# Key-value sums of four heads per product, both signs on the 128 rows and 65 columns, and one slab that reads out from normalized, transposed queries

## The chip, the cores and the metric

The kernel runs on one core of a Trainium2 chip. The metric is the device time of one launch in microseconds, as a median over several runs. A profiler has recorded one execution of the kernel before. The engines are named as the profile names them: PE is the matrix engine, PEld its weight loads, DVE, ACT and POOL are the vector, scalar and GpSimd engines, and SP is the engine whose queue issues most transfers.

## The reference, cut to what matters

The input x has 2048 rows of 512 numbers. Four blocks are added to it in turn, each on a layer-normalized x: linear attention (called layer 0), a gated feed-forward block (layer 1), attention again (layer 2), and the feed-forward block again (layer 3). Both attentions use the same weights, and so do both feed-forward blocks.

```
pq, pk  = q @ w_phi, k @ w_phi                       # 32 heads of 16 numbers each
phi_q   = concat(softmax(pq), softmax(-pq))          # 32 features per head
phi_k   = concat(softmax(pk), softmax(-pk))
kv      = sum over rows of phi_k[f] * v[d]           # 32 x 16 per head
z       = sum over rows of phi_k[f]
o       = (phi_q @ kv) / (phi_q @ z + 1e-6)
x       = x + o @ wo
x       = x + (relu(y @ W_gate) * (y @ W_up)) @ W_down     # 1376 columns between
```

## The kernel before

The 2048 rows are 16 tiles t of 128 rows, and four tiles make a slab s. Each operation is declared with its engine, its reads and writes and an assumed cost; a planner orders the operations on each engine once, by a stored list of ranks (`RANKS`) and a list of operations that go to their other engine (`MOVED`). On the chip each engine, and each DMA queue (that of SP among them), works off its own list strictly in that order and waits on semaphores. A burst of matmuls declared as one operation raises its semaphore once, at its end.

At the start, PE transposes the key and query weights (`turn`, line 579, four operations of four transposes for each, with four copies out of PSUM by ACT or DVE for each), and `compose` multiplies them with the block-diagonal w_phi. So there are weights `Wkp` and `Wqp` that give pk and pq straight from y.

`ln` (line 612) normalizes a tile to y and transposes it to yT, mostly with a DMA transpose on SP's queue (line 654).

`kv_tile(l, t)` (line 661) makes the features of the keys of one tile: four matmuls of 512 columns (lines 672 and 676), two exponentials by ACT (line 683), sums over groups of 16 by DVE (line 692; for the tiles in `POOL_Z` by POOL and DVE, lines 688 and 689), the reciprocal (line 700, or lines 697 and 698 on ACT) and the multiplication `norm` on DVE (line 701). Tile `ft` holds all 512 positive features and then all 512 negative ones. The values take four more matmuls (line 710) and one copy.

`kv_sums(l)` (line 737) multiplies the features with the values. A group is one sign and eight heads: 128 feature columns are the stationary side, and 128 value columns with one column of ones, 129, the moving side.

```
i = e.matmul(pt.ap()[:, j * 144:j * 144 + 129], ph[l, t][0].ap()[:, s, c * 128:(c + 1) * 128], va[l, t][0].ap()[:, c, 0:129],
```

That is eight matmuls per tile, 128 per attention layer. Of the products only the blocks in which the head of the feature is the head of the value are kept, by a mask in lines 753 and 756, into `kvs` (8 groups of 144 columns).

`q_chunk(l, s, c)` (line 718) makes the query's features for 128 feature columns and all 512 rows of a slab, already transposed (features on the partitions, line 725), and exponentiates them with both signs (line 729). They are not normalized.

`attn_tile(l, t)` (line 762) reads out: eight matmuls of 144 columns (line 778), of which 16 columns give the denominators and the softmax sums of the query. ACT copies these (line 792), POOL or DVE combines them (lines 799, 801, 805) with a logarithm and an exponential on ACT between (lines 803, 804), DVE scales the two signs apart (lines 815, 820), DVE or POOL adds them (lines 824, 825), the result is transposed (line 831 by PE, line 836 by a DMA) and multiplied with wo (line 841), and DVE adds it to x (line 844).

`glu_slab` and `gate_col` (line 857) make the feed-forward block's hidden columns for a slab (lines 871, 878, 879), `rem` (line 883) its last 96 columns, and `down` (line 911) the product with W_down for one tile (lines 925, 927, 933). After `down(1, t)` the kernel declares `ln(2, t)` and `kv_tile(2, t)`, so that the keys of layer 2 are made while layer 1 is still at work. All query chunks of layer 2 are declared after that.

Of the kernel before, what the change touches and what calls it, by code (L numbers as in the profile page):

```python
# [421 lines left out]
def build_kernel(nc, A_x, A_wqkv, A_w_phi, A_wo, B_x, B_W_gate, B_W_up, B_W_down, out):  # L422
# [28 lines left out]
    kvs = sb("kvs", [8, 144])  # L451
# [5 lines left out]
    p_ph = ring("phik", 16, [2, 512])  # L457
    p_va = ring("vaug", 16, [NC, 130])
    p_eq = ring("expq", 22, [512])
    p_hT = ring("hT", 22, [512])  # L460
# [7 lines left out]
    p_z = ring("z", 4, [64], FP32)  # L468
    p_rz = ring("rz", 4, [64])
# [121 lines left out]
    if ("sp", "wqn") in LOADS or ("pool", "wqn") in LOADS:  # L591
        turn(lambda ic: wqn[:, ic, :], lambda ic: [c_wqn, c_wd], t_wq, c_wqT, "WqT", ["act", "dve", "act", "dve"])
# [64 lines left out]

    ph, va = {}, {}
    kop = {}

    def kv_tile(l, t):
        src, rr = yT[l, t // 4], res("yT", l, t)
        c0 = (t % 4) * 128
        kt, kr = tile(p_ps, "K", l, t)
        ft, fr = tile(p_ph, "ph", l, t)
        zt, zr = tile(p_z, "z", l, t)
        rt, rzr = tile(p_rz, "rz", l, t)
        ph[l, t] = (ft, fr)

        def mmk(e):  # L670
            for ic in range(4):
                i = e.matmul(kt.ap(), src.ap()[:, ic, c0:c0 + 128], Wkp[:, ic, :], start=(ic == 0), stop=(ic == 3))  # L672
            return i
        if (l, t) == (0, 0):
            for ic in range(4):
                o = op("pe", lambda e, ic=ic: e.matmul(kt.ap(), src.ap()[:, ic, c0:c0 + 128], Wkp[:, ic, :], start=(ic == 0), stop=(ic == 3)),
                       reads=[rr, r_wk[ic]], writes=[kr], claims=[ft], ii=216, lat=382, name=f"K{l}.{t}")
            kop[l, t] = o
        else:
            kop[l, t] = op("pe", mmk, reads=[rr] + r_wk, writes=[kr], claims=[ft], ii=864, lat=1030, name=f"K{l}.{t}")  # L680
        fr2 = [Res("phh", ft), Res("phh", ft)]
        for s in range(2):
            op("act", lambda e, s=s: e.activation(ft.ap()[:, s, :], kt.ap(), ACT.Exp, scale=(1.0, -1.0)[s]), reads=[kr], writes=[fr2[s]], ii=477, lat=600, name=f"expk{l}.{t}")  # L683
        if (l, t) in POOL_Z:
            ht_, hr_ = tile(p_t, "zh", l, t)
            zh = lambda: ht_.ap().rearrange("p a b -> p (a b)").bitcast(FP32)
            v = lambda: ft.ap().rearrange("p s (a f b) -> p (s a) f b", f=16, b=2)
            op("pool", lambda e: e.tensor_tensor(zh().rearrange("p (a b f) -> p a f b", f=8, b=2), v()[:, :, 0:8, :], v()[:, :, 8:16, :], ALU.add), reads=fr2, writes=[hr_], ii=1110, lat=1154, name=f"Zp{l}.{t}")
            op("dve", lambda e: e.tensor_reduce(zt.ap(), zh().rearrange("p (q f) -> p q f", f=8), AX.X, ALU.add), reads=[hr_], writes=[zr], ii=590, lat=670, name=f"Zh{l}.{t}")
            zr = [zr]  # L690
        else:
            op("dve", lambda e: e.tensor_reduce(zt.ap().rearrange("p (a b) -> p a b", b=2), ft.ap().rearrange("p s (a f b) -> p (s a) b f", f=16, b=2), AX.X, ALU.add),  # L692
               reads=fr2, writes=[zr], ii=1105, lat=1185, name=f"Z{l}.{t}")
            zr = [zr]
        if (l, t) in ACT_RZ:
            lz = Res("lz", zt)
            op("act", lambda e: e.activation(zt.ap(), zt.ap(), ACT.Ln), reads=zr, writes=[lz], ii=150, lat=260, name=f"lZ{l}.{t}")
            op("act", lambda e: e.activation(rt.ap(), zt.ap(), ACT.Exp, scale=-1.0), reads=[lz], writes=[rzr], ii=150, lat=260, name=f"rZa{l}.{t}")
        else:
            op("dve", lambda e: e.reciprocal(rt.ap(), zt.ap()), reads=zr, writes=[rzr], ii=420, lat=526, name=f"rZ{l}.{t}")  # L700
        op("dve", lambda e: e.tensor_tensor(ft.ap().rearrange("p s (a f b) -> p (s a) f b", f=16, b=2), ft.ap().rearrange("p s (a f b) -> p (s a) f b", f=16, b=2),  # L701
                                            rt.ap().rearrange("p (a b) -> p a b", b=2).unsqueeze(2).to_broadcast([P, 32, 16, 2]), ALU.mult),
           reads=fr2 + [rzr], writes=[fr], ii=602, lat=695, name=f"norm{l}.{t}", port=True)
        vt, vr = tile(p_ps, "V", l, t)
        at, ar = tile(p_va, "va", l, t)
        va[l, t] = (at, ar)

        def mmv(e):
            for ic in range(4):
                i = e.matmul(vt.ap(), src.ap()[:, ic, c0:c0 + 128], wv[:, ic, :], start=(ic == 0), stop=(ic == 3))  # L710
            return i
        op("pe", mmv, reads=[rr, c_wv], writes=[vr], claims=[at], ii=864, lat=1030, name=f"V{l}.{t}")
        op_copy("act", lambda: at.ap()[:, :, 0:128], lambda: vt.ap().rearrange("p (c n) -> p c n", c=4), [vr] + ([res("va1", i) for i in range(16)] if l == 0 else []), [ar], f"va{l}.{t}", False)


    eq = {}
# [14 lines left out]


    GROUPS = [[(0, 0), (0, 1), (0, 2)], [(1, 0), (1, 1), (1, 2)], [(0, 3), (1, 3)]]
    kvr = {}
    BURSTS = [(0, 4), (4, 8), (8, 12), (12, 14), (14, 15), (15, 16)]

    def kv_sums(l):
        for b, gs in enumerate(GROUPS):
            pt, pres = tile(p_ps, "kv", l, b)
            n = len(gs)  # L740
            for q, ts in enumerate(BURSTS):
                def mm(e, gs=gs, ts=ts, pt=pt):
                    for t in range(*ts):
                        for j, (s, c) in enumerate(gs):
                            i = e.matmul(pt.ap()[:, j * 144:j * 144 + 129], ph[l, t][0].ap()[:, s, c * 128:(c + 1) * 128], va[l, t][0].ap()[:, c, 0:129],  # L745
                                         start=(t == 0 and j == 0), stop=(t == 15 and j == len(gs) - 1), skip_group_check=True)
                    return i
                k = (ts[1] - ts[0]) * n
                op("pe", mm, reads=[ph[l, t][1] for t in range(*ts)] + [va[l, t][1] for t in range(*ts)], writes=[pres], ii=k * 58, lat=k * 58 + 166, name=f"kv{l}.{b}.{q}",
                   after=[kop[l, 12]])  # L750
            g = b * 3
            src = lambda pt, n: pt.ap()[:, 0:n * 144].rearrange("p (j w) -> p j w", w=144)
            op("dve", lambda e, g=g, n=n, pt=pt: e.tensor_tensor(kvs[:, g:g + n, 0:128].rearrange("p j (h d) -> p j h d", h=8), src(pt, n)[:, :, 0:128].rearrange("p j (h d) -> p j h d", h=8),
                                                                 mask2[:].unsqueeze(1).unsqueeze(3).to_broadcast([P, n, 8, 16]), ALU.mult),
               reads=[pres, c_m2], writes=[res("kvsn", b)], ii=70 + n * 132, lat=150 + n * 132, name=f"kvs{l}.{b}")
            op("dve", lambda e, g=g, n=n, pt=pt: e.scalar_tensor_tensor(kvs[:, g:g + n, 128:136], src(pt, n)[:, :, 128:129].to_broadcast([P, n, 8]), 5e-7,
                                                                        mask2[:].unsqueeze(1).to_broadcast([P, n, 8]), ALU.add, ALU.mult),
               reads=[pres, c_m2], writes=[res("kvsd", b)], ii=90, lat=180, name=f"kvsd{l}.{b}")
        kvr[l] = [[res("kvsn", b), res("kvsd", b), res("kvsm")] for b in range(3)]


    def attn_tile(l, t):
        s4, tt = t // 4, t % 4
        st_, sr = tile(p_sm, "sm", l, t)
# [8 lines left out]
        for b, gs in enumerate(GROUPS):  # L773
            pt, pres = rb[b]

            def mm(e, gs=gs, pt=pt, b=b):
                for j, (s, c) in enumerate(gs):
                    i = e.matmul(pt.ap()[:, j * 144:(j + 1) * 144], eq[l, s4, c, s][0].ap()[:, tt * 128:(tt + 1) * 128], kvs[:, b * 3 + j, :], start=True, stop=True)  # L778
# [29 lines left out]
        for b, gs in enumerate(GROUPS):  # L808
# [16 lines left out]
           alt=("pool", lambda e: e.tensor_tensor(ot_.ap(), tt_.ap()[:, 0, :], tt_.ap()[:, 1, :], ALU.add), 1015.0, 1060.0))  # L825
        if (l, t) in PE_O:
# [6 lines left out]
            op("pe", mmt, reads=[or_] + c_id, writes=[pres], ii=230, lat=400, name=f"oTp{l}.{t}")  # L833
            op_copy("act", lambda: oT_.ap(), lambda pt=pt: pt.ap().bitcast(BF16)[:, 0:512].rearrange("p (k n) -> p k n", k=4), [pres], [oTr], f"oTcp{l}.{t}", True)
        else:
            op("sp", lambda e: e.dma_start_transpose(oT_.ap(), ot_.ap()), reads=[or_], writes=[oTr], dma="tr", nbytes=500, name=f"oT{l}.{t}")
# [105 lines left out]
    for i in range(16):  # L942
        op("pool", lambda e, i=i: e.memset(va_all[i][:, :, 128:130], 1.0), writes=[res("va1", i)], ii=60, name="vones", after=[yop[0, 0]])
# [4 lines left out]
    op("pool", lambda e: e.tensor_copy(kvs[:, :, 136:144], mask2[:].unsqueeze(1).to_broadcast([P, 8, 8])), reads=[c_m2], writes=[res("kvsm")], ii=200, lat=280, after=[kop[0, 8]], name="kvsm")  # L948
# [13 lines left out]
    for l in (0, 2):  # L962
        for s in range(NS):
            for c in range(4):
# [5 lines left out]
        for s in range(NS):  # L970
# [3 lines left out]
            for t in range(4 * s, 4 * s + 4):  # L974
                down(l + 1, t, last=(l == 2))
                if l == 0:
                    ln(2, [t])
                    kv_tile(2, t)
    pr.first([kop[0, t] for t in range(FIRST)], 1e5)
# [135 lines left out]
```

## Time and profile before

| quantity | value |
|---|---|
| median of 4 runs | 389.25 us (388.61 to 390.22) |
| the profiled execution | 388.61 us |
| its span, first to last instruction | 386.8 us |
| around the span (worked out) | 1.8 us |
| granted PE clock, mean | 1.000 |
| busy: PE, DVE, ACT, POOL | 378.0, 294.8, 195.5, 57.4 us |

A matmul's row in the profile gives its duration from start to end, and successive matmuls overlap. The time that a matmul costs PE in a stream is therefore the distance between starts: a burst's length less one duration, divided by the number of matmuls less one. Busy shares of the other engines can be read directly. The profile's tables of windows give the busy time of each engine in a stretch, in microseconds and with the number of instructions in brackets.

### The profile page before, as it was taken

The numbers are of one execution on the slowest core, as the hardware profiler recorded it, in microseconds if no ns is written. First come the engines' busy times: TensorE is split into PE (matmuls) and PEld (weight loads), VectorE is DVE, ScalarE is ACT, GpSimd is POOL, SyncE is SP. The second block draws the span as 40 slices with busy tenths as digits, with TensorE's granted clock in tenths as the row PEclk, the third lists the DMA queues.
The fourth block names the chain that finished last, engine by engine and source line by source line (L and its number), as shares of the span: only waits on it lengthen the run. The fifth ranks groups of instructions, "written<-read, shape, count | busy, mean of one in ns | idle before, by whom it ended". The sixth has DMA issues, their size and how long they took to land.

```text
span 386.8 us, 6635 instructions
## 1 busy us (share of the span) xinstructions
PE 378.0 (98%) x2430; PEld 214.0 (55%) x2471; DVE 294.8 (76%) x646; ACT 195.5 (51%) x609; POOL 57.4 (15%) x129
## 2 busy tenths in 40 slices
PE   8999899999999999999999999999999999999997
PEld 6545575787554544444444467587565454444443
DVE  7999977999997886663798986899867784643443
ACT  6999859664253236243256675875342343123210
POOL 1377301213112000000000000222201020100000
PEclk9999999999999999999999999999999999999999
DMA  8542951223232222010030100022330221210101
GB/s 254 157 97 43 297 196 30 43 55 70 54 70 54 44 54 41 15 27 2 0 69 2 27 2 1 15 43 54 70 82 18 65 56 27 74 36 14 42 14 54
DMA packets 60592, 22.89 MB, mean 59 GB/s; under 512 B 51760, under 2 KB 60304, under 8 KB 60560
## 3 DMA queue, kind: packets, MB, share of 16 engines
q1 hardware_dynamic: 57440, 19.35, 22.1%
q10 hardware_dynamic: 2832, 2.08, 1.7%
q0 software_dynamic: 288, 1.05, 0.8%
q8 instruction: 19, 0.31, 0.3%
q14 instruction: 13, 0.11, 0.1%
HBM read 8.44 MB, written 2.10 MB: 27 GB/s over the span
## 4 chain that ended last, share of the span: by engine, by line
PE 76%; DVE 10%; ACT 8%; DMA 3%; issue 1%; POOL 1%; SPq 1%; POOLq 0%
PE pb L871 32%; PE pb L925 17%; PE pb L841 5%; PE pb L725 5%; PE pb L672 4%; PE pb L710 4%; PE pb L745 3%; ACT phik L683 3%; PE pb L778 3%; PE pb L899 2%; ACT expq L729 2%; PE pb L927 2%; DVE phik L701 2%; DMA Wd<-in_A_wqkv_dram 2%; DVE t L815 1%
## 5 line engine op out<-in xcount | busy, mean ns | idle before, releaser
L878 ACT ACTIVATE gate<-pb 128x512 bf16<-128x512 f32 (+1 forms) x100 | 51.1, 512 | 76.6 <-PE pb L871 73.7
L879 DVE TENSOR_TENSOR hT<-gate,pb 128x512 bf16<-128x512 bf16 (+1 forms) x100 | 56.9, 577 | 39.3 <-PE pb L871 36.8
L871 PE MATMUL pb<-yT,Wu 128*128 128x512 bf16 (+1 forms) x396 | 82.6, 336 | 0.2
L871 PE MATMUL pb<-yT,Wg 128*128 128x512 bf16 (+1 forms) x393 | 81.7, 336 | 0.5
L925 PE MATMUL pb<-Wd,hT 128*128 128x512 bf16 (+2 forms) x322 | 75.5, 372 | 0.5
L871 PEld LDWEIGHTS pb<-yT,Wu 128*128 128x128 bf16 x400 | 38.7, 98 | 30.6 <-DVE x_sb L844 0.6
L871 PEld LDWEIGHTS pb<-yT,Wg 128*128 128x128 bf16 x400 | 38.5, 98 | 29.4 <-DVE t L820 0.3
L925 PEld LDWEIGHTS pb<-Wd,hT 128*128 128x128 bf16 x330 | 31.6, 98 | 35.3
L614 DVE BATCH_NORM_STATS2 stats<-x_sb 128x6 f32<-128x512 bf16 x64 | 43.2, 686 | 1.3 <-DMA x_sb<-in_A_x_dram 0.7
L729 ACT ACTIVATE expq<-pb 128x512 bf16<-128x512 f32 x64 | 35.3, 618 | 8.8 <-PE pb L725 8.8
L683 ACT ACTIVATE phik<-pb 128x512 bf16<-128x512 f32 x64 | 35.7, 614 | 7.1 <-PE pb L672 6.4
L815 DVE TENSOR_TENSOR t<-pb,sm 128x384 bf16<-128x384 f32 x64 | 33.5, 549 | 1.4 <-POOL sm L805 1.3
L933 DVE TENSOR_TENSOR x_sb<-x_sb,pb 128x512 bf16<-128x512 bf16 (+2 forms) x33 | 21.9, 666 | 14.4 <-PE pb L927 14.3
L623 ACT ACTIVATE lnv<-mv,eps 128x1 f32<-128x1 f32 (+1 forms) x58 | 17.3, 309 | 29.4 <-DVE mv L615 29.2
L841 PE MATMUL pb<-wo,oT 128*128 128x512 bf16 x119 | 30.9, 379 | 0.8 <-DMA oT<-o 0.5
L640 DVE TENSOR_SCALAR y<-x_sb,mv,rstd 128x512 bf16<-128x512 bf16 x63 | 28.1, 462 | 4.1 <-ACT rstd L625 3.9
L725 PE MATMUL pb<-yT,Wqp 128*128 128x512 bf16 x124 | 30.6, 379 | 0.3
L710 PE MATMUL pb<-wv,yT 128*128 128x512 bf16 x124 | 30.7, 379 | 0.2
L672 PE MATMUL pb<-Wkp,yT 128*128 128x512 bf16 x120 | 30.2, 379 | 0.5 <-DMA yT<-y 0.3
L844 DVE TENSOR_TENSOR x_sb<-x_sb,pb 128x512 bf16<-128x512 bf16 x32 | 21.8, 680 | 11.2 <-PE pb L841 10.8
L792 ACT ACTIVATE sm<-pb 128x48 f32<-128x48 f32 (+1 forms) x96 | 16.6, 217 | 20.0 <-PE pb L778 19.9
L692 DVE TENSOR_REDUCE z<-phik 128x64 f32<-128x1024 bf16 x21 | 25.0, 1201 | 1.1 <-ACT phik L683 1.1
(81 smaller groups left out, 412.2 us busy)
## 6 DMA issues: line engine op xcount, KB each, us to landing
out_dram<-x_sb ACTq DMA_DIRECT2D x15, 128.0 KB, 1.7
Wg<-in_B_W_gate_dram SPq DMA_DIRECT2D x2, 640.0 KB, 7.5
Wu<-in_B_W_up_dram SPq DMA_DIRECT2D x2, 640.0 KB, 8.5
Wd<-in_B_W_down_dram SPq DMA_DIRECT2D x1, 1280.0 KB, 12.3
x_sb<-in_A_x_dram POOLq DMA_DIRECT2D x2, 512.0 KB, 4.8
yT<-y SPq DMA_TRANSPOSE x55, 2.5
Wd<-in_A_wqkv_dram SPq DMA_DIRECT2D x2, 256.0 KB, 3.2
Wd<-in_A_wqkv_dram SPq DMA_DIRECT2D x1, 512.0 KB, 5.9
```

The source lines that it names most:

```text
L614: op("dve", lambda e, t=t: e.bn_stats(stats[:, t, :], x_sb[:, t, :]), reads=[res("x", t)], writes=[res("st", t)], ii=600, lat=690, name=f" ...
L672: i = e.matmul(kt.ap(), src.ap()[:, ic, c0:c0 + 128], Wkp[:, ic, :], start=(ic == 0), stop=(ic == 3))
L683: op("act", lambda e, s=s: e.activation(ft.ap()[:, s, :], kt.ap(), ACT.Exp, scale=(1.0, -1.0)[s]), reads=[kr], writes=[fr2[s]], ii=477, la ...
L710: i = e.matmul(vt.ap(), src.ap()[:, ic, c0:c0 + 128], wv[:, ic, :], start=(ic == 0), stop=(ic == 3))
L725: i = e.matmul(qt.ap(), Wqp[:, ic, c * 128:(c + 1) * 128], src.ap()[:, ic, :], start=(ic == 0), stop=(ic == 3))
L729: op("act", lambda e, g=g: e.activation(es[g][0].ap(), qt.ap(), ACT.Exp, scale=(1.0, -1.0)[g]), reads=[qr], writes=[es[g][1]], ii=477, lat ...
L815: return e.tensor_tensor(tt_.ap()[:, b, 0:384].rearrange("p (c h d) -> p c h d", h=8, d=16), pt.ap()[:, 0:432].rearrange("p (c w) -> p c w ...
L841: i = e.matmul(wt.ap(), oT_.ap()[:, c, :], wo[:, c, :], start=(c == 0), stop=(c == 3))
L871: i = e.matmul(pt.ap()[:, 0:n], W[:, ic, fc * 128:(fc + 1) * 128], src.ap()[:, ic, a * 128:b * 128], start=(ic == 0), stop=(ic == 3))
L878: op("act", lambda e: e.activation(st_.ap()[:, 0:n], gt.ap()[:, 0:n], ACT.Relu), reads=[gr], writes=[sr], ii=110 + n * .72, lat=230 + n * ...
L879: op("dve", lambda e: e.tensor_tensor(ht.ap()[:, a * 128:b * 128], st_.ap()[:, 0:n], ut.ap()[:, 0:n], ALU.mult), reads=[sr, ur], writes=[h ...
L925: i = e.matmul(pt.ap()[:, 0:n1 - n0], hT[l, s, fc].ap()[:, c:c + 128], Wd[:, fc, n0:n1], start=(fc == 0), stop=False)
```

## The change

The feature tile is laid out anew: eight groups of four heads, and in each group 64 positive and then 64 negative features. One group's 128 columns therefore hold both signs of four heads, and they meet only the 64 value columns of these heads and one column of ones, 65. `kv_sums` keeps its count of eight matmuls per tile. The blocks on the diagonal are now written by DVE in instructions on 64 partitions into `kvs`, which POOL clears once; `q_chunk` and `attn_tile` stay as they were for every slab but one.

For the slab in `NQ`, the first of layer 2, the queries are made like the keys: `q_tile` runs the new `features` (the body of `kv_tile` moved out) with `Wqp`, so that the query's features are normalized, and two DMA transposes on SP's queue per tile turn them. They are declared right after `kv_tile(2, t)`. `attn_tile_n` then reads out with eight matmuls of 68 columns against `kvn`: 64 numerators and four denominators, and DVE divides. The exponentials' sums for these four tiles are begun on POOL (`POOL_Z` has `("Q", 2, t)`).

The query weights are transposed by four DMA transposes on SP's queue (`WQ_DMA`) in place of PE and copies. The buffers of `expq` and `hT` become one pool of 40, and `phik` has 18 buffers. `RANKS` and `MOVED` are new; `PAIR_Z` is empty. Cut to its core:

```diff
-    p_ph = ring("phik", 16, [2, 512])
-    p_va = ring("vaug", 16, [NC, 130])
-    p_eq = ring("expq", 22, [512])
-    p_hT = ring("hT", 22, [512])
+    p_ph = ring("phik", 18, [8, 2, 64])
+    p_va = ring("vaug", 16, [8, 66])
+    p_eq = ring("expq", 40 if ONE else 22, [512])
+    p_hT = p_eq if ONE else ring("hT", 22, [512])
...
+        if WQ_DMA:
+            for ic in range(4):
+                op("sp", lambda e, ic=ic: e.dma_start_transpose(t_wq.ap()[:, :, ic * 128:(ic + 1) * 128], wqn[:, ic, :]), reads=[c_wqn, c_wd], writes=[c_wqT[ic]], dma="tr", nbytes=500, name="WqT",
+                   after=chain["sp"][-1:])
...
+    def q_tile(l, t):
+
+        ft, fr = tile(p_ph, "pq", l, t)
+        qs = [tile(p_eq, "qT", l, t, b) for b in range(2)]
+        features("Q", l, t, Wqp, r_wq, ft, fr, [ft] + [x[0] for x in qs])
+        for b in range(2):
+            op("sp", lambda e, b=b: e.dma_start_transpose(qs[b][0].ap().rearrange("p (k n) -> p k n", k=4), ft.ap().rearrange("p g s f -> p (g s f)")[:, 512 * b:512 * b + 512]), reads=[fr], writes=[qs[b][1]],
+               dma="tr", nbytes=500, name=f"qT{l}.{t}.{b}")
...
-                            i = e.matmul(pt.ap()[:, j * 144:j * 144 + 129], ph[l, t][0].ap()[:, s, c * 128:(c + 1) * 128], va[l, t][0].ap()[:, c, 0:129],
+                            i = e.matmul(pt.ap()[:, j * 66:j * 66 + 65], ph[l, t][0].ap()[:, g].rearrange("p s f -> p (s f)"), va[l, t][0].ap()[:, g, 0:65],
...
+            if any((l, s) in NQ for s in range(NS)):
+                op("dve", ... kvn[:, hh:8:2, 0:64] ... [P, 4, 4, 16] ...)
+                op("dve", ... kvn[:, hh:8:2, 64:68] ... [P, 4, 4] ...)
+            for s in range(2):
+                op("dve", ... kvs[pd, s * 4:s * 4 + 4, hh * 64:hh * 64 + 64] ... [64, 4, 4, 16] ...)
+                op("dve", ... kvs[pd, s * 4:s * 4 + 4, 128 + 4 * hh:132 + 4 * hh] ... [64, 4, 4] ...)
...
+    def attn_tile_n(l, t):
+                for j in range(4):
+                    i = e.matmul(pt.ap()[:, j * 68:(j + 1) * 68], qT[l, t][b][0].ap()[:, j * 128:(j + 1) * 128], kvn[:, 4 * b + j, :], start=True, stop=True)
+            op("act", ... lnd ... ACT.Ln)                      # once for each b
+        op("act", lambda e: e.activation(rden(), lnd(), ACT.Exp, scale=-1.0), ...)
+            op("dve", ... ot_ = pt * rden ... [P, 4, 4, 16])   # once for each b
...
+    op("pool", ... mask4 ...)
+    op("pool", lambda e: e.memset(kvs[:].rearrange("p j w -> p (j w)"), 0.0), ...)
...
-POOL_Z = {(0, t) for t in range(3, 14)}
+WQ_DMA = True
+PAIR_Z = set()
+KV_AFTER = 12
+ONE = True
+LAG = 3
+NQ = {(2, 0)}
+POOL_Z = {(0, t) for t in range(1, 13)} | {("Q", 2, t) for t in range(4)}
```

## The prediction

> **What bounds the kernel now.** I read the page's busy shares first, then the groups by shape, then the order of time on PE around the two places where key-value sums run, and last the busy time by stage.
>
> ```profile
> PE 378.0 (98%) x2430; PEld 214.0 (55%) x2471; DVE 294.8 (76%) x646; ACT 195.5 (51%) x609; POOL 57.4 (15%) x129
> ...
> PE   8999899999999999999999999999999999999997
> ```
>
> PE looks full, but its rows overlap, so this alone proves nothing. What counts is the distance between starts. These bursts show it:
>
> ```profile
> 4.67 1.06 PE L586 MATMUL pb<-ident,Wd 128*128 128x128 bf16 x16
> ...
> 202.42 1.03 PE L725 MATMUL pb<-yT,Wqp 128*128 128x512 bf16 x4
> ...
> 45.87 5.72 PE L745 MATMUL pb<-vaug,phik 128*128 128x129 bf16 x96 [1.34 <-DVE phik L701]
> ...
> 232.63 4.56 PE L745 MATMUL pb<-vaug,phik 128*128 128x129 bf16 x76
> ...
> 52.29 1.16 PE L778 MATMUL pb<-kvs,expq 128*128 128x144 bf16 x16
> ```
>
> A burst less one duration, over its matmuls less one: 128 columns (1.06-0.219)/15 = 56.1 ns; 144 columns (1.16-0.226)/15 = 62.3; 512 columns (1.03-0.379)/3 = 217; and 129 columns (5.72-0.220)/95 = 57.9 in layer 0 and (4.56-0.220)/75 = 57.9 in layer 2. From the code there are 1344 matmuls of 512 columns, 320 of 256, 128 of 192, 256 of 144, 256 of 129 and some 170 of 128. At 216, 109, 82, 62.5, 57.9 and 56 ns (35 of the last come first and slower, 3.84 us) they take 290.3 + 34.9 + 10.5 + 16.0 + 14.8 + 11.4 = 378 us of a span of 386.8. The 9 us left are the start, the end, and one idle stretch of 1.34 us before the sums of layer 0. So PE's issue is the bound nearly everywhere, and what is taken from it is time, unless another engine comes up beside it. Where one could is seen in the stages:
>
> ```profile
> 0.00:45.90 45.90, 42.17 (x292) 24.18 (x298) 43.39 (x103) 40.63 (x113) 22.91 (x52) 1.00 0.58 158
> 45.90:70.00 24.10, 23.81 (x227) 15.92 (x231) 19.71 (x51) 19.08 (x69) 2.92 (x10) 1.00 0.41 129
> 70.00:130.00 60.00, 59.55 (x422) 38.24 (x427) 54.16 (x136) 28.03 (x108) 13.07 (x22) 1.00 0.31 58
> 130.00:196.00 66.00, 65.68 (x322) 31.16 (x327) 45.54 (x88) 23.56 (x63) 0.64 (x2) 1.00 0.14 28
> 196.00:225.50 29.50, 29.34 (x141) 13.55 (x143) 27.38 (x45) 20.74 (x52) 0.00 (x0) 1.00 0.12 23
> 225.50:256.00 30.50, 30.10 (x281) 19.85 (x283) 24.02 (x56) 21.20 (x72) 4.62 (x13) 1.00 0.05 10
> 256.00:276.00 20.00, 19.43 (x171) 15.37 (x172) 18.41 (x48) 11.39 (x46) 5.58 (x14) 1.00 0.34 61
> ```
>
> After the length come PE, PEld, DVE, ACT and POOL. DVE is 95% full up to 45.9 us, 93% from 196 to 225.5 and 92% from 256 to 276, and has a third free from 130 to 196.
>
> **The change, part by part.**
>
> *Key-value sums: 256 matmuls from 129 to 65 columns.* No row has fewer than 128 columns. Upper bound of the new price: 57.9 ns, if something other than columns sets it; lower: the line through 128 and 512 columns, (217-56.1)/384 = 0.419 ns a column, gives 56.1-63*0.419 = 29.7. Each matmul has its own weight load, so that could set it. These rows speak of loads:
>
> ```profile
> L745 PEld LDWEIGHTS pb<-vaug,phik 128*128 128x128 bf16 x256 | 15.0, 97 | 2.5 <-DVE phik L701 2.1
> ...
> 55.22 0.11 PEld L725 LDWEIGHTS pb<-yT,Wqp 128*128 128x128 bf16 x2 [0.53 <-DVE t L820]
> ```
>
> One load lasts 97 ns, yet two together last 0.11 us: the second starts some 15 ns after the first, and the 97 ns are mostly passage. A load per 30 ns has a precedent for a pair, none for a stream. A rule speaks against the change here: the Trainium skill ("TensorE: Matmul & The Clock Gate", "Back-to-back issue gap") gives a real stream of load and matmul about 81 ns at 128 columns, more than the columns take. Held as a fixed extra of 25 ns over 56, it would make 65 columns 55 ns, and the sums would save 256*3 = 0.7 us. But this trace has 56.1 at 128 with a load for each matmul, so the extra isn't there. I take 31 ns (129 columns lie 1.4 ns over the line; so may 65): saving 256*26.9 = 6.9 us, between 0 and 7.2. In layer 0, 96 matmuls of it stand behind the last `norm`; in layer 2, 76.
>
> *Read-out of four tiles: 32 matmuls from 144 to 68 columns*, 31.0 ns by the line against 62.3: 1.0 us, between 0 and 1.0.
>
> *Query weights by DMA.* PE loses 16 transposes at 56 ns, 0.9 us; ACT and DVE four copies, at 615 and 415 ns about 2.1 us. SP gets four transposes. A yT transpose took 1.29 us to issue, so 5.2 us; they wait for the query weights, which PE's transposes before the change found at 9.1 us, and SP's list has nothing between 4.7 and 15.28 us, when the first yT transpose goes. They end at about 14.3: hidden. Were the weights 2 us later, the yT transposes queued behind would be as late, then `kv_tile`'s matmuls and ACT, at most 1 to 2 us. The first query chunk stood at 37.5 us, so 16 us of slack cover the later `Wqp`.
>
> *Head of layer 0.* One tile more has its sums begun by POOL: DVE 1201 to 674 ns, -0.5, with two DVE copies gone -0.8: 1.3 us off an engine that ended the stage (PE's wait of 1.34 us names `norm`, L701). POOL adds 1.3 for the sum and some 1.1 for clearing and masks to 22.9 busy of 45.9: covered. So the stage ends about 1.3 us earlier, and PE's 0.9 and part of its wait go with it.
>
> *Writing kvs.* Before: two instructions of 551, one of 416 and three of about 175 ns per layer, 2.05 us. After, in layer 0: four of 256 elements and four small ones. The nearest row is 128x256 at 416 ns; half the partitions I price the same (below 0.2 or above 0.5 there is no reason): 4*(0.416+0.175) = 2.4. In layer 2 `kvn` adds 1.2: 3.6. PE does query chunks meanwhile (48 of its matmuls, 10.4 us, stood behind the sums both times), and for the first slab of layer 2 only the 1.2 lie ahead. Both signs now need both banks; that costs one chunk's time, which is filler. If that filler were spent earlier, 0.3 and up to 1.5 us would show.
>
> *Queries of the first slab.* PE's 16 matmuls of 512 columns (3.46 us) and ACT's eight exponentials move from around 202 to 225 us to about 130 to 170; none is removed. New there, per tile: POOL 1307 ns, DVE 674 + 681 = 1.4 us, ACT 2*258 ns, SP two issues of 1.2 us. Per slab DVE gets 5.4 us where it has 20 free, ACT 2.1, SP 9.5 us of 66. A qT transpose waits for `norm`; behind it on SP stand the yT transposes of layer 2, hence keys, but PE has feed-forward matmuls to spare there. Gone per tile at 240 to 275 us: DVE 2*549 + 418 + 418 and the `sm` steps, against two of 416: 4.4 us for the slab; ACT three copies of about 215 for one logarithm. Net DVE there 4.4-1.5 = 2.9 us lighter. With a shorter chain (POOL's steps drop out), the 0.6 us that PE waits at 273 us may go.
>
> *Sum.* PE's work falls by 6.9 + 1.0 + 0.9 = 8.8 us. Idle time: about 1 us less in the head and around 273; against it I set 1 us of new waits, since around 196 to 230 DVE stays at 93% while PE loses 3.46 us of filler. Span 386.8-8.8 = 378.0, plus 1.8 outside: 379.8 for an execution like the profiled one. That one lies 0.64 under the median, so 380.4; I say **380.5**.
>
> **Rivals.**
>
> *A: the short matmuls don't shorten.* If a pair of load and matmul costs a fixed time near 50 ns, the sums give 256*8 = 2.0, the read-out 0.4, the weights 0.9: 386; at no gain, 388.5. For it: no stream here is faster than 55 ns, and the rule quoted. Against: the 15 ns between two loads, and a straight line from 512 to 128 columns.
>
> *B: gains partly swallowed by DVE.* From 196 to 276 us PE loses 3.46 moved + 3.4 in sums + 1.0 = 7.9 us of work, DVE 2.9 of work and perhaps 3.4 of waiting for the sums (it is idle about 4.6 us from 230 to 240). If DVE holds the stage, it shortens by 6.3, while PE pays 3.46 more before 196: net 2.8 in place of 4.4. With 4 in layer 0 that is 382.5; if layer 0's exponentials on ACT (19.1 of 24.1 busy) hold too, 384.
>
> *C, slower: the moved queries stand bare.* At 130 to 170 us PE is full, so 3.46 us are added there at once. If the stage from 219 to 256 can't close up because the last `norm` and the chain to the first feed-forward matmul set its length, nothing is given back. This wins over all the rest once a short matmul costs above some 48 ns: 288*(58-48) = 2.9 and 0.9 for the weights just cover 3.46. At 57: 389.25 + 3.46 - 0.9 - 0.3 = 391.5. For it: DVE's 93%; against: PE had query chunks of other slabs to fill with.
>
> That the change doesn't do what it says I exclude by counting: eight matmuls per tile before and after, every product kept is still made.
>
> **How the numbers follow.** Main case 0.66 (378 to 383); B 0.16 (382 to 385.5); A 0.10 (385.5 to 388.5); C 0.08 (389 to 392). Range 376.5 to 387: it leaves out C and the end of A, and below it reaches to 7.2 + 1.0 + 0.9 with 2 to 3 us of idle time gone as well. A measurement of this kernel can tell 0.3% (1.2 us) from no change. Faster: main, B and most of A, 0.88; same 0.04; slower 0.08.
>
> **What would show it.** Right: the sums at about 31 ns a matmul, and their last burst in layer 0 near 2.9 us where 5.7 stood; the read-out of tiles 0 to 3 near 31; PE's waits of over 0.5 us no more than before; SP's four weight transposes over by 15 us. Wrong: a distance of 50 or more between starts (A), PE waiting on DVE between 196 and 276 us for more than 2 us (B), or the sums starting as late as before though 3.46 us went ahead (C).

## The result, and the profile after

The changed kernel takes 387.39 us (median of 32 runs) against 389.18 (53 runs): a ratio of 0.9951, 95% interval 0.9941 to 0.9961. It is faster, by 1.8 us, where the prediction had 8.8. Its first profiled execution ran at a lower granted clock than its other runs, so the lines below are of a second profile of the same kernel, with a span of 384.6 us.

Busy shares and the slices of PE, of the changed kernel's page:

```profile
PE 371.1 (96%) x2412; PEld 205.1 (53%) x2455; DVE 289.9 (75%) x638; ACT 201.9 (52%) x619; POOL 60.5 (16%) x126
...
PE   7699999899999999999999999999999999999997
```

Each digit is a fortieth of the span, 9.6 us. PE's row began with 8 9 9 9 8; now the first 19 us read 7 and 6. What the sums and the new read-out cost is seen in the groups by shape and, below them, in the timeline of the changed kernel:

```profile
L786 PE MATMUL pb<-vaug,phik 128*128 128x65 bf16 x256 | 8.7, 192 | 0.1
```

```profile
50.77 2.23 PE L786 MATMUL pb<-vaug,phik 128*128 128x65 bf16 x64
...
227.91 1.13 PE L786 MATMUL pb<-vaug,phik 128*128 128x65 bf16 x32
...
241.28 0.67 PE L901 MATMUL pb<-kvn,expq 128*128 128x68 bf16 x16
```

A burst less one duration, over its matmuls less one: (2.23 - 0.19)/63 = 32 ns, (1.13 - 0.19)/31 = 30 ns, and 32 ns for 68 columns. Over all starts that follow closely, 65 columns have a mean of 30.3. So the work went away as forecast. Where did the time go? Busy time by the same stages as before (length, PE, PEld, DVE, ACT, POOL, clock, DMA):

```profile
0.00:45.90 45.90, 39.14 (x257) 21.15 (x262) 39.03 (x96) 37.00 (x102) 24.41 (x52) 0.96 0.71 167
45.90:70.00 24.10, 22.62 (x226) 12.79 (x226) 19.45 (x47) 21.50 (x71) 4.62 (x12) 1.00 0.40 128
70.00:130.00 60.00, 59.11 (x439) 39.34 (x446) 54.99 (x140) 30.39 (x118) 10.72 (x26) 1.00 0.30 60
130.00:196.00 66.00, 65.68 (x317) 30.90 (x322) 38.48 (x77) 19.23 (x51) 1.80 (x3) 1.00 0.14 29
196.00:225.50 29.50, 29.34 (x138) 13.48 (x140) 29.09 (x46) 25.55 (x71) 2.32 (x2) 1.00 0.20 41
```

In the first 45.9 us PE was busy 3 us less than before and DVE 4.4 less, and yet the first GLU (feed-forward) matmul of layer 1 came later, at 72.6 us for 69.9. The granted clock of the first stage is 0.96 where it was 1.00. Ten microseconds each, first of the kernel before, then of the changed one, show where:

```profile
10.00:20.00 10.00, 9.95 (x72) 5.51 (x71) 9.80 (x25) 10.00 (x27) 4.25 (x9) 1.00 0.52 148
20.00:30.00 10.00, 9.65 (x44) 4.23 (x44) 10.00 (x22) 10.00 (x29) 6.97 (x14) 1.00 0.51 102
...
10.00:20.00 10.00, 6.08 (x41) 3.08 (x42) 8.84 (x22) 6.46 (x18) 4.98 (x8) 1.00 1.14 205
20.00:30.00 10.00, 9.95 (x43) 4.46 (x42) 7.05 (x19) 8.48 (x24) 5.73 (x11) 0.83 0.40 80
```

From 10 to 20 us PE waits, and from 20 to 30 us it works at a clock of 0.83. The trace has the clock at one half from 20.93 to 24.34 us, and PE is busy all that while, so it loses 1.7 us there that no wait shows. PE's two longest waits in the first 75 us (us in total, times, longest), then, from the timeline, the two bursts around the longer of them:

```profile
PE pb L606 <- DMA yT<-Wd: 2.1, 1, 2.1
PE pb L739 <- DMA wv<-in_A_wqkv_dram: 1.7, 1, 1.7
```

```profile
16.95 0.61 PE L606 MATMUL pb<-BD,yT 128*128 128x128 bf16 x8
...
19.70 0.40 PE L606 MATMUL pb<-BD,yT 128*128 128x128 bf16 x4 [2.15 <-DMA yT<-Wd]
```

`yT<-Wd` is a transposed query weight. L606 is `compose`, and it stands in PE's list ahead of values and keys. In the kernel before, all of PE's waits for transfers up to 45.9 us came to 0.6 us; here, with 0.4 for the weights themselves, they come to 4.2.

A ledger says the same in one table. For each point I take its time in the trace, and the work of all PE instructions that stand ahead of it in the list, priced at full clock (216 ns for 512 columns, 57.9 or 30 for a sum, and so on). The difference is called PE's idle time up to there; the 1.7 us that the half clock took are in it.

| point | before: time, work, idle | changed: time, work, idle |
|---|---|---|
| first sum of layer 0 | 35.6, 31.2, 4.5 | 45.2, 34.5, 10.6 |
| last sum of layer 0 | 51.4, 45.5, 5.9 | 52.8, 41.8, 11.0 |
| first GLU matmul of layer 1 | 69.9, 63.1, 6.8 | 72.6, 58.7, 13.9 |
| last sum of layer 2 | 237.0, 230.1, 6.9 | 240.4, 226.3, 14.1 |
| first GLU matmul of layer 3 | 255.5, 247.7, 7.8 | 254.5, 239.3, 15.2 |
| end | 384.3, 376.0, 8.3 | 382.1, 366.8, 15.3 |

PE's work fell by 9.2 us and its idle time rose by 7.0. All of this rise is there by the first GLU matmul, at 72.6 us, and 6.1 of it by the first sum; behind 72.6 us nothing is lost. From it to the first GLU matmul of layer 3 the kernel went from 185.6 to 181.9 us, 3.7 less where the prediction had 4.4 for that part.

### The profile page after: what moved, and what is told of

Read it like the earlier page. It is cut to its first block, busy times and chain, and to the rows that moved or that the text cites. A ratio compares the mean times of both kernels' runs of the same rounds, so it can differ in the third digit from the quotient of the medians.

```text
span 400.6 us, 6617 instructions
## 1 busy us (share of the span) xinstructions
PE 385.4 (96%) x2412; PEld 211.1 (53%) x2455; DVE 293.1 (73%) x638; ACT 203.8 (51%) x619; POOL 61.6 (15%) x126
## 4 chain that ended last, share of the span: by engine, by line
PE 79%; DVE 7%; ACT 6%; DMA 5%; issue 1%; SPq 1%; POOL 0%; POOLq 0%; ACTq 0%
PE pb L966 33%; PE pb L1020 17%; PE pb L936 7%; PE pb L682 5%; PE pb L739 5%; DMA yT<-Wd 3%; PE pb L837 3%; ACT phik L695 3%; PE pb L994 3%; PE pb L754 2%; PE pb L1022 2%; DVE phik L708 2%; DMA Wd<-in_A_wqkv_dram 1%; PE pb L786 1%; ACT expq L758 1%
## 5 line engine op out<-in xcount | busy, mean ns | idle before, releaser
L974 DVE TENSOR_TENSOR expq<-gate,pb 128x512 bf16<-128x512 bf16 (+1 forms) x100 | 57.1, 577 | 41.1 <-PE pb L966 40.3
L1020 PE MATMUL pb<-Wd,expq 128*128 128x512 bf16 (+2 forms) x320 | 77.8, 383 | 0.5
L966 PEld LDWEIGHTS pb<-yT,Wu 128*128 128x128 bf16 x400 | 39.7, 100 | 31.2
L1020 PEld LDWEIGHTS pb<-Wd,expq 128*128 128x128 bf16 x330 | 32.4, 100 | 37.2 <-ACT gate L973 0.3
L695 ACT ACTIVATE phik<-pb 128x512 bf16<-128x512 f32 x72 | 39.0, 612 | 3.8 <-PE pb L682 3.8
L700 POOL TENSOR_TENSOR t<-phik 128x512 f32<-128x512 bf16 x16 | 22.5, 1412 | 91.3 <-ACT phik L695 89.7
L739 PE MATMUL pb<-wv,yT 128*128 128x512 bf16 x124 | 33.9, 405 | 0.4 <-issue 0.2
L758 ACT ACTIVATE expq<-pb 128x512 bf16<-128x512 f32 x56 | 31.4, 616 | 5.0 <-PE pb L754 5.0
L682 PE MATMUL pb<-Wkp,yT 128*128 128x512 bf16 x122 | 31.2, 394 | 0.1
L874 DVE TENSOR_TENSOR t<-pb,sm 128x384 bf16<-128x384 f32 x56 | 29.8, 550 | 1.0 <-POOL sm L864 0.9
L754 PE MATMUL pb<-yT,Wqp 128*128 128x512 bf16 x107 | 27.4, 389 | 0.3
L851 ACT ACTIVATE sm<-pb 128x48 f32<-128x48 f32 (+1 forms) x84 | 14.6, 216 | 23.4 <-PE pb L837 23.2
```

Of the source, the lines that this page charges most:

```text
L682: i = e.matmul(kt.ap(), src.ap()[:, ic, c0:c0 + 128], W[:, ic, :], start=(ic == 0), stop=(ic == 3))
L695: op("act", lambda e, s=s: e.activation(ft.ap()[:, :, s, :], kt.ap().rearrange("p (g f) -> p g f", f=64), ACT.Exp, scale=(1.0, -1.0)[s]), ...
L754: i = e.matmul(qt.ap(), Wqp[:, ic, c * 128:(c + 1) * 128], src.ap()[:, ic, :], start=(ic == 0), stop=(ic == 3))
L758: op("act", lambda e, g=g: e.activation(es[g][0].ap(), qt.ap(), ACT.Exp, scale=(1.0, -1.0)[g]), reads=[qr], writes=[es[g][1]], ii=477, lat ...
L874: return e.tensor_tensor(tt_.ap()[:, b, 0:384].rearrange("p (c h d) -> p c h d", h=8, d=16), pt.ap()[:, 0:432].rearrange("p (c w) -> p c w ...
L966: i = e.matmul(pt.ap()[:, 0:n], W[:, ic, fc * 128:(fc + 1) * 128], src.ap()[:, ic, a * 128:b * 128], start=(ic == 0), stop=(ic == 3))
```

## The experiments

Three theories were tried, in this order: the query weights by DMA hold up the head, the part up to layer 0's last sum (W); VectorE's norms, not PE, end the stage of the sums (D); the copies of the sums, which now need both banks, stand bare, with no work of PE beside them (theory C, not the prediction's rival C). P is the prediction's own step: each ns off a sum is a ns off the time. Times of kernels are medians; the kernel before was at 389.1 to 389.4 us beside them. "In the changed order" means that an experiment keeps the changed kernel's list of each engine, "in the order of before" that it keeps the old one.

**The query weights: after_again, wq_on_pe, compose_late, before_wq_dma.** The changed kernel once more (387.65); the weights turned on PE again, all else in the changed order (387.52, ratio 0.9943 to 0.9967):

```
-WQ_DMA = True
+WQ_DMA = False
```

In compose_late the DMA transposes stay and only PE's `Wqp` matmuls move back in its list; they begin at 24.2 us instead of 17.0 (386.34, 0.9906 to 0.9941). before_wq_dma is the kernel before with its query weights turned by DMA, and with `compose` for them where the changed kernel has it (393.5, 1.0102 to 1.0131):

```
-turn(lambda ic: wqn[:, ic, :], ..., t_wq, c_wqT, "WqT", ["act", "dve", "act", "dve"])
+for ic in range(4):
+    op("sp", lambda e, ic=ic: e.dma_start_transpose(t_wq.ap()[:, :, ic * 128:(ic + 1) * 128], wqn[:, ic, :]), ...)
```

> The changed kernel once more, for an undisturbed profile. Both theories: 386 to 388 us. PE waits some 6 us at about 16 us for the transposes of the query weights, and the granted clock is about half for some microseconds after it; the 65-column matmuls stand 29 to 31 ns apart.

> The changed kernel with the query weights transposed by PE as before (16 transposes, four copies on ACT and DVE); the order of everything else on each engine is kept. Theory W (the loss is the wait for the DMA transposes of the weights and what it draws after it: late rows of x, a halved clock): the wait goes, PE idles under 1.5 us between 10 and 45 us, granted clock 1.00, time 379 to 381.5 us, 0.975 to 0.98 of the kernel before. Rival B (DVE holds the later stages and swallows what PE gains): 384.5 to 386.5 us, with PE waiting on DVE between 196 and 276 us.

> The changed kernel with the DMA transposes of the weights kept, and the four operations of compose for the queries put behind the values of tile 4 in PE's list, so that PE reaches them about 5 us later; the order of the rest is kept. Theory W1 (only the place in PE's list costs): 380 to 382.5 us. Theory W2 (the transposes and the loads of x, 8 to 15, slow one another on the shared DMA engines, so rows of x and the yT transposes behind are late as well): the wait of PE appears again at the keys of tile 4, whose yT lands near 22 us, and the time is 384.5 to 387.5 us.

> The kernel before with one part of the change: the query weights are transposed by four DMAs on SP's queue, and compose stands where the changed kernel has it. Theory W: slower by what the change lost, 394 to 398 us, the loads of x 8 to 15 landing 3 to 5 us later than in the kernel before, PE idle for 5 to 7 us near 16 us. Rival B: the same as before within 1.5 us, 388 to 391 us.

In the order of before the edit costs 4.3 us, where the prediction had it gain 0.9. Landings in before_wq_dma, median us from issue (the last number):

```profile
x_sb<-in_A_x_dram POOLq DMA_DIRECT2D x2, 512.0 KB, 5.4
...
yT<-y SPq DMA_TRANSPOSE x6, 2.5
yT<-Wd SPq DMA_TRANSPOSE x4, 4.7
```

These four transposes run while the last rows of x arrive, and land after 4.7 us where those of `yT` take 2.5. But the planner had made another order for the changed kernel, and there taking them out gains nothing. Moving their reader gains 1.1 in the medians, with intervals that just touch. In compose_late the wait only changes its name, and in wq_on_pe, without the transposes, PE waits for other transfers (the second fence, as totals):

```profile
20.25 1.04 PE L682 MATMUL pb<-Wkp,yT 128*128 128x512 bf16 x4 [3.00 <-DMA yT<-y]
```

```profile
PE pb L682 <- DMA yT<-y: 2.0, 4, 1.2
...
PE pb L587 <- DMA Wd<-in_A_wqkv_dram: 1.5, 2, 0.9
```

after_again and the six experiments in the changed order show 3.3 to 4.3 us of such waits up to 45.9 us in their profiles, whichever of the weights' edits they carry; before it is 0.6.

So W is true of the edit, and explains at most about 1 us of the 7 in the order that the changed kernel has.

**The short sums alone: kv_only and kv_clear_late.** The kernel before with its order; new are the sums of 65 columns and their copies, and GpSimd's clearing of `kvs`, at 6 us in one and at 45 in the other:

```
-WQ_DMA = True
+WQ_DMA = False
...
-NQ = {(2, 0)}
+NQ = set()
-POOL_Z = {(0, t) for t in range(1, 13)} | {("Q", 2, t) for t in range(4)}
+POOL_Z = {(0, t) for t in range(3, 14)}
```

> The kernel before with its order, its query weights turned on TensorE and its old first slab of queries; new are the 65-column key-value sums and their copies alone (the clearing of kvs is put on GpSimd at the start, ahead of the loads it issues). The prediction's step (every ns saved on these matmuls and on the reads shortens the path): about 389.2 - 6.9 + 0.4 for the copies = 382 to 383. Rival D (VectorE's last norm ends each layer's sums, and only the matmuls behind it are on the path: the last sum follows the last norm by 1.35 us in layer 0 and by 1.9 in layer 2, and would follow by about 0.3): 1.0 + 1.6 less, 0.4 back: 386 to 388. The last norm of layer 0 should end at 50.0 us by both.

> kv_only with GpSimd's clearing of kvs moved behind its last half-sum of layer 0 (43 us) instead of ahead of its loads. If clearing at 6 us held up the loads (the query weights landed at 10.5 us in kv_only, at 9.1 in the kernel before): 389.3, 1.4 us less than kv_only. If the loads only land differently from one execution to the next: 390.5, within 0.5 of kv_only. In both the copies of kvs, now behind both banks, keep their 1.7 us per layer.

They took 390.75 (1.0025 to 1.0049) and 390.25 (1.0018 to 1.0042): with about 7 us of PE's work gone, and with no moved query, the kernel is slower than before. Both theories had forecast a gain. The place of the clearing makes no difference that can be told. The timeline of kv_clear_late at the end of layer 0's sums:

```profile
48.45 1.14 PE L786 MATMUL pb<-vaug,phik 128*128 128x65 bf16 x32 [0.66 <-DVE phik L708]
...
50.26 0.42 PE L786 MATMUL pb<-vaug,phik 128*128 128x65 bf16 x8 [0.66 <-DVE phik L708]
...
50.86 0.90 PE L786 MATMUL pb<-vaug,phik 128*128 128x65 bf16 x24 [0.18 <-DVE phik L708]
...
51.80 0.87 DVE L809 TENSOR_TENSOR kvs<-pb,mask 64x256 bf16<-64x256 f32 x2 [0.99 <-PE pb L786]
...
51.81 0.81 PE L754 MATMUL pb<-yT,Wqp 128*128 128x512 bf16 x3
...
52.70 0.36 DVE L812 SCALAR_TENSOR_TENSOR kvs<-pb,mask 64x16 bf16<-64x16 f32 x2
...
53.09 0.89 DVE L809 TENSOR_TENSOR kvs<-pb,mask 64x256 bf16<-64x256 f32 x2
...
53.12 0.36 PE L837 MATMUL pb<-kvs,expq 128*128 128x144 bf16 x3 [0.49 <-DVE kvs L812]
...
54.01 0.39 DVE L812 SCALAR_TENSOR_TENSOR kvs<-pb,mask 64x16 bf16<-64x16 f32 x2
...
54.45 0.99 PE L837 MATMUL pb<-kvs,expq 128*128 128x144 bf16 x13 [0.97 <-DVE kvs L812]
```

Two things are seen here. First, PE waits for norms (L708) before every burst. The last norm ends at 50.80 and the last sum starts at 51.57; before, these were 50.02 and 51.37. Only this tail, 1.35 against 0.77 us, could become shorter. The norms came 0.8 later because the query weights landed 6.7 us after their issue in this profile and 5.9 in that of before: in the profiles with the old order, PE's transposes and all norms, the last norm follows this landing (50.0 us at 5.9, 50.4 at 6.3, 50.8 at 6.7, 51.5 at 7.3). Second, the copies. Before, there were three banks whose sums ended one after the other, so their copies ran beside the sums still under way:

```profile
50.81 0.55 DVE L753 TENSOR_TENSOR kvs<-pb,mask 128x384 bf16<-128x384 f32 x1
...
51.50 0.88 DVE L753 TENSOR_TENSOR kvs<-pb,mask 128x384 bf16<-128x384 f32 x2
...
52.30 0.17 DVE L756 SCALAR_TENSOR_TENSOR kvs<-pb,mask 128x16 bf16<-128x16 f32 x1
```

They were done 1.1 us after the start of the last sum. Now eight copies start when both banks are done and end 2.8 us after it, and the three chunk matmuls in PE's list (0.81 us) do not cover that. From the last sum to the first GLU matmul of layer 1, kv_clear_late takes 20.3 us and the kernel before 18.5. In layer 2 the shorter sums save 1.9 us and the copies cost 1.7.

**The copies by themselves: half_copies.** kv_clear_late without the four instructions per layer that write the second sign's half of `kvs`:

```
-for s in range(2):
+for s in range(1):
     ps_, pd = slice(64 * s, 64 * s + 64), slice(64 * hh, 64 * hh + 64)
```

> kv_clear_late without the four instructions per layer that write the second sign's half of kvs (that half stays zero; all matmuls stay). If the copies stand bare between the last sum and the read-out (theory C: 2 x (0.43 + 0.18) = 1.2 us per layer): 2.4 us under kv_clear_late. If TensorE's query chunks cover them, as the prediction had it: within 0.3 of kv_clear_late in layer 0, and at most 0.5 in all.

387.76 against 390.25: 2.5 us for eight instructions, 2.4 expected. From layer 2's last sum to the first GLU matmul of layer 3 it takes 1.15 us less, which is the full price. In layer 0 the same stretch gives 0.66, but in this profile PE's clock was at one half from 50.7 to 54.1 us, over the last sums and the copies, so the price there is known from the times alone. Theory C holds in this order, and the cover that the prediction named does not.

**The norms: before_head, norms_out_head, norms_out_late.** before_head has the whole change but for the weights and the choice of tiles whose sums POOL begins, with the order of before for all that starts in the first 69 us, and with the clearing at 6 us; the other two leave out four norms of layer 0, in that order and in compose_late's:

```
 for k in ((t - 1, t) if pair else (t,)):
-    norms[l, k]()
+    if (kind, l, k) not in SKIP:      # SKIP = {("K", 0, t) for t in range(4, 8)}
+        norms[l, k]()
```

> The whole change but for the query weights (turned on TensorE as before) with the order of the kernel before for all that starts in the first 69 us (layer 0's norms, keys, features, sums), and the order of the changed kernel behind it. If the changed kernel's loss sits in its order of the first 70 us: the GLU of layer 1 starts at about 69.5 us instead of 72.6, the stage behind it keeps its 181.6 us and the end its 129.0: 382 to 383.5. If the loss is the new operations themselves (masks, clears, copies): 386 to 388.

> before_head without the norms of tiles 4 to 7 of layer 0 (their features stay unscaled; four instructions of 0.62 us on VectorE, 2.5 us). If VectorE's chain ends the head in this order (47.4 of the first 50.9 us): the last norm 2 us earlier and the time 385. If TensorE or the loads end it: 387, within 0.5.

> compose_late without the same four norms. In this order TensorE has no gap from 37 to 49 us and the doubled sums cost their full length, so TensorE should hold the head: 386.0 to 386.4, a gain of at most 0.6 where the last sums wait 0.4 us for a norm. If VectorE holds it here too: 384.3.

before_head took 387.11 (0.9937 to 0.9961): its first GLU matmul is at 72.3 us, not at 69.5. The old order of the head brings nothing back: with the short sums it loses as much, by waits for norms (2.1 us), by bare copies and, in this profile, by a clock of one half from 48.6 to 52.1 us. norms_out_head took 386.0 (0.9909 to 0.9941), 1.1 less than before_head where 2 was expected. norms_out_late took 386.11 (0.9888 to 0.9939), which can't be told from compose_late. So in the old order norms hold the head in part; in the changed one nothing of it is seen, within some 1 us.

**Doubled sums: kv_twice and kv_twice_first.** 252 of the 256 sums are issued twice in the changed kernel, or 126 of layer 0's 128 in kv_clear_late (the traces have 254 for each doubled layer):

```
+if t or j:
+    e.matmul(pt.ap()[:, 264 + j * 60:324 + j * 60], ph[l, t][0].ap()[:, g]..., va[l, t][0].ap()[:, g, 0:60], start=False, ...)
 i = e.matmul(pt.ap()[:, j * 66:j * 66 + 65], ...
```

> The changed kernel with 255 of its 256 key-value matmuls issued a second time, 60 columns each into unused columns of the same bank; the same order otherwise; 255 x 28 to 29 ns = 7.2 us more work of TensorE. The prediction's step (these matmuls are on the path): 387.4 + 7.2 = 394 to 395, each layer's sums ending 3.6 us later. Rival D (VectorE's last norm ends them; a burst that stands ahead of the last norms costs nothing): layer 0's sums end 0.3 to 1 us later, layer 2's 1 to 3.6 later, 389 to 392.

> kv_clear_late (order of before) with layer 0's 127 of 128 key-value matmuls issued a second time, 60 columns each: 3.6 us more of TensorE's work, 1.8 of it in the bursts of tiles 0 to 7 at 36 and 45 us, and 1.8 in tiles 8 to 15, of which 8 matmuls stand behind the last norm. If VectorE's norms end the stage in this order: up to 0.5 us later (390.3 to 390.8). If TensorE's work is the bound (the prediction's step): 393.8.

kv_twice took 394.23, 6.8 us more than the changed kernel for 7.2 of work, with 3.6 by layer 0's last sum and 3.2 in layer 2. That is P's number, and D falls for this order: PE starts the stage late, with 10.6 us already idle, and from there to the last sum it waits less than 1 us in all, so longer sums cost their full length. Even the last norm ends 1.7 us later, at 54.3. That shorter sums gain as much isn't shown by this. kv_twice_first took 392.41, 2.2 more for 3.6 of work, though its last norm ended at 50.5, no later than in kv_clear_late: PE's waits for norms fell from 2.9 to 1.4 us, and the rest shows. But 1.6 of these 2.2 us is one gap among the sums, for which the profile names no releaser. Without it the last sum would come some 0.6 us later than in kv_clear_late, which is D's number. So this run doesn't decide between P and D.

**Clearing early, and one copy for two.** clear_early is compose_late with GpSimd's clearing of `kvs` at 6 us instead of 40:

> compose_late with GpSimd's clearing of the key-value matrix (memset 1.06 us, and the mask's copy) moved from 38 us to about 7 us. If VectorE's norms near it were stretched by it (five norms of 5.0 us where four take 2.5): the last norm of layer 0 ends 1 us earlier and the time falls to 385.3. If it was hidden: 386.3 as compose_late, within 0.5.

386.73 against 386.34: nothing gained. Its profile had the full clock and a wait of 3.6 us for `yT`, and came to its first sum at 45.3 us, where the changed kernel had 45.2. one_copy is compose_late with 17 columns for each head (16 values and the denominator), so that one instruction copies both; the 5e-7 added to each denominator is left out:

```
-p_va = ring("vaug", 16, [8, 66])
+p_va = ring("vaug", 16, [8, 68])
-    e.tensor_tensor(kvs[pd, ..., hh * 64:hh * 64 + 64]...)          # 64x256
-    e.scalar_tensor_tensor(kvs[pd, ..., 128 + 4 * hh:132 + 4 * hh]...)  # 64x16
+    e.tensor_tensor(kvs[pd, ..., hh * 72:hh * 72 + 72]....rearrange("p j (h w) -> p j h w", w=18)[:, :, :, 0:17], ...)  # 64x272
```

> compose_late with values and denominator of each head side by side (17 columns a head, 68 a group instead of 65): one copy instruction of 272 elements for each of the four quarters of kvs, and for each half of kvn, instead of two; the 5e-7 added to each denominator is left out. Theory C: each small copy saved is 0.18 to 0.2 us bare, 4 in layer 0 and up to 2 in front of layer 2's read-out: 0.9 to 1.1 us, less 256 x 1.3 ns = 0.3 for three more columns: 385.6. If query chunks cover the copies in this order: 386.3 to 386.7.

```profile
53.58 1.86 DVE L803 TENSOR_TENSOR kvs<-pb,mask 64x272 bf16<-64x272 f32 x4 [0.40 <-PE pb L786]
```

385.58 us (0.989 to 0.9947), 0.8 less than compose_late, whose interval overlaps; and three of its eight runs had a full clock, none of compose_late's six. So the times alone don't show a gain. The stage does: from the last sum to the first GLU matmul of layer 1 it takes 19.19 us, and 19.81 or 19.82 in five profiles of this order with the two copies; in layer 2 13.86 for 14.14 or 14.15. These 0.9 us are what theory C expected.

> before_head with the same one copy in place of two, and with the clearing of kvs behind GpSimd's last half-sum (43 us). Theory C: the copies are barer in this order (R after the last sum by 1.55 us, and 8.8 us to the first output projection where before has 7.2), so 4 x 0.2 in layer 0 and 2 x 0.2 in layer 2: 1.0 to 1.2 less, 0.3 more for the columns: 386.2. If covered: 387.1 to 387.5.

This one tests nothing: the kernel that ran still has the two copies, so it is only before_head with the clearing moved to 46 us, and its 387.68 stands beside before_head's 387.11.

## Why the prediction was wrong, point by point

The step that failed is the idle time in the sum: "about 1 us less in the head and around 273; against it I set 1 us of new waits". PE's work fell by 9.2 us, a little more than the 8.8 forecast, but its idle time rose by 7.0 instead of standing still, all of it ahead of 72.6 us. In the profile that is 3.6 us more of waits for transfers and 1.7 us of half clock before the first sum, and 2 us between the last sum and the first GLU matmul; within the sums it is 1 us less. Point by point:

- **Pace of the sums and of the read-out: right.** 31 ns set, 30 to 32 measured, and no fixed cost for a weight load with each. Rival A is out, and so, for this stream, is the rule of some 81 ns for load and matmul at 128 columns that the prediction cites from the Trainium skill ("TensorE: Matmul & The Clock Gate", "Back-to-back issue gap"): 56.1 ns were measured there.
- **"In layer 0, 96 matmuls of it stand behind the last norm": misread.** The burst of 96 from 45.87 us began when ten of sixteen norms were done and ran beside the last six, until 1.35 us behind the last. The wait named in front of it was for an earlier norm. In the old order the short sums cut that tail by 0.6 us (1.35 to 0.77), not by the 2.6 that 96 sums would give; in layer 2 they saved 1.9 of some 3.5. The head was counted as PE's because PE looked full; it was full of sums that had time.
- **Writing `kvs`: price right, cover wrong.** 2.4 us per layer were set, and four instructions each of 0.42 and 0.17 us are just that. "PE does query chunks meanwhile" was the fault. What counts is where the copies begin, not how long they are: before, they began ahead of the last sum, now behind both banks. The "0.3 and up to 1.5" kept for this was 1.8 in the old order's layer 0 and 1.7 in its layer 2. In the changed order PE's idle time grows by 2.9 us from layer 0's last sum to the first GLU matmul, before by 0.9; one_copy shows 0.6 of it to be copies. In layer 2 the cover nearly holds there (0.9 before, 1.1 after), as only `kvn`'s part lies ahead.
- **Query weights by DMA: wrong in two places.** The issue took 5.5 us, near the 5.2 forecast, but it began at 10.2 instead of 9.1, and landing took 5.2 us (median), where a `yT` transpose took 2.5 before. And "16 us of slack cover the later `Wqp`" looked at its reader, the query chunk at 37 us; the matmuls that make `Wqp` stood at 17 us in PE's list, with keys and values behind them. Price: 4.3 us in the old order, at most about 1.1 in the new.
- **Head of layer 0, "1.3 us earlier": wrong.** DVE's work fell, and yet the last norm ended at 52.5 instead of 50.0: up to it DVE had nothing to do for 6.9 us, against 2.5 before. PE, late after its waits for DMA and its half clock, is the likely reason; norms_out_late agrees with it.
- **Queries of the first slab: right in sum, wrong in place.** They didn't go to 130 to 170 us but behind 194, where DVE is now 99% full (29.09 of 29.5), and PE hardly waited (0.4 us): 3.7 us gained of 4.4.
- **Rivals.** B asked for PE's waits on DVE between 196 and 276 us, the prediction's C for moved queries that stand bare; the ledger has neither. The loss was ahead of 73 us, where the prediction had a gain of 4, "at most 1 to 2 us" for late weights and a line on ACT.
- **The clock: not thought of.** The kernel before had a mean granted clock of 0.999 or 1.000 in all 55 of its executions beside the experiments. Of the changed kernel's, 4 had 1.000 (median 386.3 us), 24 had 0.995 or 0.996 (387.2) and 14 had 0.991 (388.1). One stretch of 3.4 us at one half makes 0.996 of a span of 385 us. So about 1 us of the 7 goes with the clock in a typical execution. No experiment set the clock, so this is a relation and not a shown cause.

What stays open is why the head loses in every order that was tried. In the profile shown, 5.3 of the 6.1 us by which PE's idle time has grown at its first sum are found: 4.2 us of waits for transfers against 0.6 before, and 1.7 us of half clock. But no experiment gave them back: taking the weights' transposes out or moving their reader brought other waits, and clear_early, with the full clock, was no earlier at its first sum. Of the 2 us behind the last sum, 0.6 are shown to be copies. The two profiles of the changed kernel had the query weights land 5.8 and 7.0 us after their issue, so about 1 us of any such comparison is chance. And the kernels with the old head order lose their gain in yet another way (norms, then copies); whether some order avoids both wasn't found.

## What to carry to other kernels

Before you take a burst of matmuls as standing behind a wait, count which of its inputs were ready when it started: a burst that ends shortly behind its last input can end earlier by no more than that tail, however long it is. When an accumulation is cut into other banks, look at when the copies out of them can begin, since a stage that copied bank by bank beside its matmuls becomes one that copies at the end. An operation moved to a DMA needs slack up to the first instruction in order that reads it, not up to the last use of its result. And when busy time has gone and the time has not, look at the granted clock beside the waits: here half a clock for 3.4 us hid in rows that read as busy.

## What the runs showed of the hardware that was not expected

- Four transposes from SBUF to SBUF, issued while loads of x were under way, took 4.7 to 7.3 us (the median of the four) from issue to landing in eight profiles; those of `yT`, later, 2.5 to 2.6.
- A 512 KB load issued at about 3.2 us landed after 5.3 to 7.3 us over the profiles, in two of one kernel after 5.8 and 7.0.
- A stream of load and matmul pairs ran at 28.5 ns for 60 columns, 30.3 for 65 and 31.9 for 68 (means of the distances between starts).
- PE's granted clock was at one half for 3.41 us, once, in seven profiles of kernels with the change or a part of it, and never in that of before. In five of them it came during, or within 1.3 us after, a wait of PE of 2.1 to 3.7 us. clear_early had a wait of 3.6 us and no such stretch.
- On VectorE a copy from PSUM of 64x16 took 172 ns and one of 64x256 took 420; a 64x272 copy that does both took 441.
